# Pooled attention and MLP mixer on one core: column tiles for token tails, one more 7-product unit, more turns through HBM, K/V sums in two passes

## The chip, the core and the metric

The kernel runs on one core of a Trainium2 chip. TensorE (PE; its weight loads are PEld), VectorE (DVE), ScalarE (ACT), GpSimd (POOL) and SyncE (SP) each run their own instruction list in order and wait for each other through semaphores. The metric is the device time of one execution in microseconds (us).

## The reference

Eight batches; q, k, v of 8 heads, 576 rows, 64 columns. Attention against keys and values that are means over 8 rows, then a token mixer and a channel mixer:

```
k_p, v_p = mean over 8 rows of k, v                     # 72 rows each
attn = softmax(q @ k_p^T / sqrt(64)) @ v_p              # 576 x 64 per head
x = heads side by side                                  # 8 x 576 x 512
h = relu(x^T @ w_tok1) @ w_tok2                         # 576 -> 256 -> 576 over tokens
u = x + h^T
out = u + relu(u @ w_ch1) @ w_ch2                       # 512 -> 1536 -> 512
```

Inputs and output are float32; products run in bf16.

## The kernel before

The 576 tokens of a batch are split in 512 (4 chunks of 128) and a tail of 64. The channel mixer of the 512 runs in a *unit* per batch (units 0 to 7); the tails of all batches together make unit 8. A unit is a generator that yields every few matmuls; `PLANS[n]` lists, at each yield, which other steps are issued there: the attention and token mixer of the next batch, loads of later batches, sums. `HEAD` lists the steps before unit 0. The order of each engine's instructions is exactly this order of issue.

Names of the steps, for batch b:

- `lk lq lv` issue the loads from POOL's DMA queue. K and V of batches 1 to 3 come in one load as bf16. For batches from 4 on (`SUMMED = 4`), `+k` and `+v` (`add_rows`, L145) add further rows of a pooling group onto the first ones as the data land in float32: 4 passes of 2 rows each.
- `k0 k1 v0 v1` (DVE) and `K0 K1 V0 V1` (POOL) finish the pooled sums of half the heads, by `pool8` (L214 to L223: three additions) or for the summed batches one addition (L277). `kq0 kq1 vp0 vp1` do it on PE, as 8 matmuls with the identity that add up (L323).
- `kpT` transposes pooled K on PE and copies it out (L283, L285). `Q0 Q1` transpose q in 32 x 32 blocks on DVE (L345). `s0 s1 s2` are the scores (L357): four tiles of 32 rows of PE's array. `av0` to `av4` are attention times V (L391, L395, L396); `at0 at1` and `u0` to `u4` the token mixer (L453, L468, L470). `u4` does the tails of two batches at once: `w_tok2t` holds the tail's weights twice, padded with zeros, so that four matmuls of 128 x 128 weights fill two halves of one PSUM bank.
- u must then be turned for the channel mixer (`uT`). `t0` to `t3` (DVE evacuates) and `r0` to `r3` (ACT evacuates) do it by PE transposes, four per chunk (L480, L481). For batches from `BOUNCED = 6` on, `M0 M2` write u to HBM (L488), `M` reads it back in another order into the tile `v` (L494), both from SP, and `T0` to `T3` (L499) transpose blocks on DVE.

A unit's channel mixer has a first stage (`l1_tiles`, L561, relu on ACT L564) and a second. In units 0 and 1 the second stage is plain: 48 matmuls of 512 columns (L592). From `FAST = 2` on, the second stage is a Strassen-like form with 7 products of 12 matmuls of 256 columns (`unit_fast`, L777), which needs sums of blocks of w_ch2 (`W`, L664), sums of blocks of the relu output `GT` (`=`, `g_sums`, L614 and L625), and one DVE output per product (L799). In units 3 to 8 parts of the first stage are in such a form too (`first_fast`, L695), with sums of w_ch1 (`%`) and of uT (`^`, `token_sum`). All these sums run on DVE. `ps_one` has 4 PSUM banks, `ps_two` two pairs.

The head runs 26 matmuls on zeros (L862) ahead of batch 0's first transposes.

Of the kernel before, what the change touches and what calls it, by code (L numbers as in the profile page):

```python
# [14 lines left out]
SUMMED = 4  # L15
BOUNCED = 6
FAST = 2
# [11 lines left out]
PLANS = {  # L29
# [32 lines left out]
def kernel(  # L62
# [44 lines left out]
    w_tok2t = singles.tile([P, 2, 2, P], BF16)  # L107
# [29 lines left out]
    def pair_sums(b, key):  # L137
        return loaded[b, key].rearrange("j h i d -> j (h i d)").bitcast(FP32)[:, 0:H * 2 * D].rearrange(
            "j (h n) -> j h n", h=H)

    def add_rows(b, key):
        i = parts_of[b, key]
        parts_of[b, key] = i + 1
        src = (k if key == "k" else v)[b].rearrange("h (j i) d -> j h (i d)", i=POOL)
        nc.gpsimd.dma_start(out=pair_sums(b, key), in_=src[:, :, 2 * i * D:2 * (i + 1) * D],  # L145
                            accum_op=ALU.add if i else ALU.bypass)

    def load_kv(b, src, key):
        t = loaded[b, key] = raw.tile([SP, H, POOL, D], BF16, name=key + "r")
        if b >= SUMMED:  # L150
# [31 lines left out]
    def permute_tok2(m):  # L182
# [5 lines left out]
        for half in range(2):  # L188
            nc.gpsimd.tensor_copy(out=w_tok2t[:, :, half, half * BP:(half + 1) * BP], in_=w_tok2[:, :, 8 * BP:S])
# [48 lines left out]
    def batch_steps(b):  # L238
# [26 lines left out]
        def pool(eng, t, g):  # L265
            def go():
                hs = slice(g * HP, (g + 1) * HP)
                dst = st["kp"][:, g] if t == "k" else st["vp"][:, hs, 0:D]
                if b < SUMMED:
                    pool8(eng, loaded[b, t], hs, dst, t == "k")  # L270
                    return
                pair = pair_sums(b, t)[:, hs].rearrange("j l (i n) -> i j l n", i=2)
# [7 lines left out]
        def kpT():  # L280
# [4 lines left out]
            nc.vector.tensor_copy(out=st["kD"].rearrange("p g e j -> p (g e j)"), in_=ps.rearrange("p i j -> p (i j)"))  # L285
# [47 lines left out]
        def qT(hp):  # L333
            def go():
# [4 lines left out]
                nc.vector.tensor_copy(out=qT0[:, hp].rearrange("m l (r p) -> m r l p", p=BP), in_=ps)  # L339
# [118 lines left out]
        def u(c):  # L458
            def go():
                ps = ps_one.tile([P, 512], FP32, name="p1")  # L460
                if c < 4:
                    mms = [(w_tok2[:, m, c * P:(c + 1) * P], st["AT"][:, m, :]) for m in range(2)]
                    dst, x = late("u")[:, c, :], st["x"][:, c, :]
                else:
                    mms = [(w_tok2t[:, m, half, :], tails[b // 2, half][:, m, :]) for half in range(2) for m in range(2)]
                    dst, x = u_tails[:, b // 2, :], st["xt"]
                for i, (w, a) in enumerate(mms):
                    nc.tensor.matmul(out=ps, lhsT=w, rhs=a, start=(i == 0), stop=(i == len(mms) - 1))  # L468
# [54 lines left out]
        name = {"kpT": kpT}  # L523
# [11 lines left out]
        for hp in range(HP):  # L535
            name[f"kp{hp}"], name[f"kt{hp}"] = kp2(hp, False), kt2(hp, False)
            name[f"kP{hp}"], name[f"kT{hp}"] = kp2(hp, True), kt2(hp, True)
# [75 lines left out]
    def sub(out, a, b):  # L613
        nc.vector.tensor_tensor(out=out, in0=a, in1=b, op=ALU.subtract)  # L614

    def g_sums(s):
# [5 lines left out]
        if s[0] == "3":  # L622
            sub(S4[:, 2, f], GT[:, f, lo], GT[:, f, hi])
        elif s[0] == "1":
            nc.vector.tensor_tensor(out=S4[:, 0, f], in0=GT[:, f, hi], in1=GT[:, sec, hi], op=ALU.add)  # L625
        elif s[0] == "2":
            sub(S4[:, 1, f], S4[:, 0, f], GT[:, f, lo])
        else:
            sub(S4[:, 3, f], GT[:, sec, lo], S4[:, 1, f])
# [43 lines left out]
    def token_sum(n, u, i):  # L673
# [3 lines left out]
        sub(t[:, i], a, b)  # L677
# [92 lines left out]
    def unit_fast(n, u):  # L770
# [33 lines left out]
        def store_part(cols):  # L804
            def go(i):
                if i == 0:
                    return
                for half in range(2):
                    dst = out.rearrange("(c h) (p r) n -> h p c r n", h=2, r=BR)[half]
                    (nc.scalar if half else nc.sync).dma_start(out=dst[:, 2:4, 8, cols],  # L810
                                                               in_=ob[half * BP:(half + 1) * BP, :, cols])
            return go
# [23 lines left out]
        s2 = keep("s1")  # L836
        yield from product(x, lambda m: SG[:, 1, m], lambda m: TW[:, 1, m], False,
                           plus(s2, x, u1hi), last)
        if not last:
            w = bank()  # L840
            s4 = keep("s4")
            yield from product(w, lambda m: GT[:, NH + m, hi], lambda m: TW[:, 3, m], True, plus(s4, w, u2lo))
        yield from product(z, lambda m: SG[:, 3, m], lambda m: w_ch2[:, NH + m, hi], False, plus(oa[:, :, hi], z, s2))
        store(n, 0, oa)
        if last:
            yield from product(x, lambda m: SG[:, 2, m], lambda m: TW[:, 2, m], False,
                               plus(ob[:, :, hi], x, s5, store_part(hi)), True)
            yield from product(x, lambda m: GT[:, NH + m, hi], lambda m: TW[:, 3, m], False,
                               plus(ob[:, :, lo], x, u2lo, store_part(lo)), True)
# [118 lines left out]
```

## Time and profile before

| | |
|---|---|
| three runs | 270.61, 270.71, 271.94 us; median 270.71 |
| span of the profiled execution | 269.8 us (first to last instruction) |
| granted TensorE clock | 1.000 |
| PE, DVE, ACT, POOL busy | 259.5, 206.8, 122.7, 113.4 us |
| start of units 0 to 8 | 23.45, 58.85, 89.14, 119.1, 146.4, 175.3, 205.3, 226.9, 245.9 us |
| last matmul ends | 264.6 us |

The page gives no time of its own for the profiled execution beside its span; the median lies 0.9 us above the span. Busy time of PE includes the latency of a matmul, so the spacing of matmuls in the chain of waits is the better measure of their cost. Lines are numbered as in the kernel before.

### The profile page before, as it was taken

The page shows a single profiled execution, that of the slowest core. Times are in us where ns is not written, and L with a number is a line of the kernel's source. Part 1 is how long each engine was busy: PE and PEld are TensorE (multiplying, and loading weights), DVE is VectorE, ACT ScalarE, POOL GpSimd, SP SyncE. Part 2 cuts the span into 40 slices and gives each one's busy share as a digit, 9 for nine tenths or more (in the row PEclk, how much of TensorE's full clock was granted, in tenths as well). Part 3 has the DMA queues.
Part 4 walks back from the last instruction along what each step waited for, and adds up shares of the span by engine and source line. Part 5 has one row for each costly group of instructions (what it writes and reads, how often), then busy time and mean ns, then how long its engine had stood idle before and what let it go on. Part 6 is the DMA issues. An engine that isn't in the chain of part 4 may idle for free.

```text
span 269.8 us, 5432 instructions
## 1 busy us (share of the span) xinstructions
PE 259.5 (96%) x2173; PEld 171.7 (64%) x2200; DVE 206.8 (77%) x427; ACT 122.7 (45%) x207; POOL 113.4 (42%) x114
## 2 busy tenths in 40 slices
PE   8999999999999999999999999999999999999992
PEld 2776454545544645776587657864785688787781
DVE  4755573751798859996978798899799889997981
ACT  1375773047444353736563637264922632613600
POOL 5847749999995428636657242420000000000000
PEclk9999999999999999999999999999999999999999
DMA  7999999959969898998995997361506510404106
GB/s 184 190 194 205 204 212 204 180 126 190 153 132 140 154 159 118 146 169 168 155 141 83 156 213 87 39 164 40 119 0 147 149 18 21 137 2 116 41 2 157
DMA packets 42081, 35.17 MB, mean 130 GB/s; under 512 B 12040, under 2 KB 34408, under 8 KB 42056
## 3 DMA queue, kind: packets, MB, share of 16 engines
q0 software_dynamic: 30672, 22.11, 55.3%
q1 hardware_dynamic: 11056, 12.39, 17.2%
q10 hardware_dynamic: 328, 0.33, 0.5%
q8 instruction: 17, 0.28, 0.4%
q14 instruction: 8, 0.07, 0.1%
HBM read 36.90 MB, written 10.49 MB: 176 GB/s over the span
## 4 chain that ended last, share of the span: by engine, by line
PE 90%; DVE 5%; ACT 2%; issue 1%; DVEq 0%
PE p L777 24%; PE p L561 22%; PE p L695 9%; PE p L592 8%; PE p L453 6%; PE p L468 5%; PE p L357 4%; PE p L391 3%; PE p L862 3%; PE p L480 2%; PE p L323 1%; DVE area L614 1%; DVE u L470 1%; ACT ex L379 1%; ACT x L426 1%
## 5 line engine op out<-in xcount | busy, mean ns | idle before, releaser
L564 ACT ACTIVATE GT<-p 128x512 bf16<-128x512 f32 x76 | 44.5, 596 | 57.6 <-PE p L561 43.7
L561 PE MATMUL p<-uT,w_ch 128*128 128x512 bf16 x274 | 69.3, 380 | 0.9 <-issue 0.4
L561 PEld LDWEIGHTS <-w_ch 128*128 128x128 bf16 x304 | 32.4, 114 | 24.1 <-issue 1.7
L362 ACT ACTIVATE ex<-p 72x1024 bf16<-72x1024 f32 (+1 forms) x42 | 31.6, 804 | 27.5 <-PE p L357 27.3
L777 PEld LDWEIGHTS <-area 128*128 128x128 bf16 x336 | 31.9, 98 | 5.3 <-issue 1.3
L777 PE MATMUL p<-area,area 128*128 128x256 bf16 x252 | 30.8, 273 | 0.0
L145 POOL DMA_DIRECT2D kr<-in_k_dram x16 | 23.4, 1495 | 15.6 <-DMA kr<-in_k_dram 15.6
L145 POOL DMA_DIRECT2D vr<-in_v_dram x16 | 23.1, 1478 | 14.2 <-DMA vr<-in_v_dram 14.2
L470 DVE TENSOR_TENSOR u<-p,x 128x512 bf16<-128x512 f32 x32 | 21.1, 680 | 8.2 <-PE p L468 8.2
L777 PEld LDWEIGHTS <-GT 128*128 128x128 bf16 x252 | 24.2, 98 | 4.9 <-issue 0.6
L592 PE MATMUL p<-w_ch,GT 128*128 128x512 bf16 x92 | 23.6, 379 | 0.2
L777 PE MATMUL p<-w_ch,GT 128*128 128x256 bf16 x168 | 20.6, 273 | 0.1
L799 DVE TENSOR_TENSOR o<-p,s 128x512 f32<-128x512 f32 (+1 forms) x28 | 17.9, 662 | 3.2 <-PE p L777 3.1
L396 DVE TENSOR_TENSOR x<-p,den 128x512 bf16<-128x512 f32 x28 | 19.4, 691 | 1.0
L468 PE MATMUL p<-AT,w_tok 128*128 128x512 bf16 x62 | 17.3, 379 | 0.5 <-DVE u L470 0.5
L799 DVE TENSOR_TENSOR s<-p,u 128x512 f32<-128x512 f32 x24 | 16.2, 680 | 2.0 <-PE p L777 2.0
L395 DVE RECIPROCAL den<-p 128x8 f32<-128x8 f32 (+1 forms) x35 | 7.0, 201 | 11.3 <-PE p L391 10.9
L391 PEld LDWEIGHTS <-ex 72*128 72x128 bf16 x280 | 12.6, 98 | 3.9 <-DVE x L396 0.2
L592 PEld LDWEIGHTS <-GT 128*128 128x128 bf16 x96 | 8.8, 98 | 9.4 <-issue 0.4
L453 PE MATMUL p<-x,w_tok 128*128 128x512 bf16 x53 | 13.7, 379 | 0.2
L446 ACT ACTIVATE AT<-p 128x512 bf16<-128x512 f32 x14 | 8.4, 597 | 12.1 <-PE p L453 11.7
L391 PE MATMUL p<-vp,ex 72*128 72x65 bf16 x280 | 13.7, 194 | 0.0
(151 smaller groups left out, 448.8 us busy)
## 6 DMA issues: line engine op xcount, KB each, us to landing
out_dram<-o SPq DMA_DIRECT2D x34, 256.0 KB, 3.8
kr<-in_k_dram POOLq DMA_DIRECT2D x16, 288.0 KB, 7.4
vr<-in_v_dram POOLq DMA_DIRECT2D x16, 288.0 KB, 7.0
qb<-in_q_dram POOLq DMA_DIRECT2D x7, 576.0 KB, 10.1
kr<-in_k_dram POOLq DMA_DIRECT2D x3, 576.0 KB, 10.9
vr<-in_v_dram POOLq DMA_DIRECT2D x3, 576.0 KB, 12.4
w_ch<-in_moe_w_ch_dram POOLq DMA_DIRECT2D x6, 256.0 KB, 10.6
w_ch<-in_moe_w_ch_dram POOLq DMA_DIRECT2D x3, 512.0 KB, 13.1
```

Of the source, the lines that this page charges most:

```text
L145: nc.gpsimd.dma_start(out=pair_sums(b, key), in_=src[:, :, 2 * i * D:2 * (i + 1) * D], accum_op=ALU.add if i else ALU.bypass)
L362: nc.scalar.activation(out=exv[:, a, :, gs[0]:gs[-1] + 1, n0:n0 + n], func=AF.Exp, scale=scale, in_=pss[a][0:SP, :, 0:len(gs) * n].rearran ...
L391: nc.tensor.matmul(out=ps[:, h // 4, (h % 4) * (D + 1):(h % 4 + 1) * (D + 1)], lhsT=st["ex"][:, h * S + n0:h * S + n0 + P], rhs=st["vp"][: ...
L453: nc.tensor.matmul(out=ps, lhsT=w_tok1[:, c if c < 4 else 4 + par, m * P:(m + 1) * P], rhs=st["x"][:, c, :] if c < 4 else st["xt"], start= ...
L468: nc.tensor.matmul(out=ps, lhsT=w, rhs=a, start=(i == 0), stop=(i == len(mms) - 1))
L470: nc.vector.tensor_tensor(out=quads_of(dst, on), in0=plain_of(ps, on), in1=plain_of(x, on), op=ALU.add)
L561: nc.tensor.matmul(out=ps[m], lhsT=w_ch1[m // 4][:, kk, m % 4:512:4], rhs=moving(u)[kk], start=(kk == 0), stop=(kk == 3))
L564: nc.scalar.activation(out=GT[:, m, :], in_=ps[m], func=AF.Relu)
L592: nc.tensor.matmul(out=ps, lhsT=GT[:, m, c * P:(c + 1) * P], rhs=w_ch2[:, m, :], start=(m == 0), stop=(m == NM - 1))
L695: nc.tensor.matmul(out=ps[:, i], lhsT=w(i, k), rhs=mv(k), start=start and (i, k) == (0, 0), stop=stop and k == 1, skip_group_check=True)
L777: nc.tensor.matmul(out=ps[i] if split else ps[:, i], lhsT=a(m)[:, i * P:(i + 1) * P], rhs=w(m), start=start and m == 0 and (i == 0 or spli ...
L799: nc.vector.tensor_tensor(out=dst, in0=src, in1=other[:, i], op=ALU.add)
```

## The change

`BOUNCED` becomes 3 (batches 3, 4, 5 are turned through HBM too, in units 2, 3, 4), `FAST` becomes 1 (unit 1's second stage gets 7 products), and `ROWS` says that K and V of batches 4 to 7 are summed in 2 passes of 4 rows; one more addition then joins the halves. `PLANS` and `HEAD` are written anew, with batches named outright (`k1:2` is step k1 of batch 2); `#` is a GT sum on POOL instead of DVE, `~` a token sum on POOL, `kpA` is `kpT` with ACT evacuating, `p0` to `p3` are q transposes that ACT evacuates. K of batch 1 is pooled by `K0:1` (POOL, end of the head) and `k1:1` (DVE, unit 0), that of batches 2 and 3 by `k0 k1` (DVE, units 0 and 1). The head loads K and q in smaller alternating pieces from SP and has 13 matmuls on zeros. The second stage's products stand in a new order, and the last unit stores its results in smaller pieces.

```diff
-SUMMED = 4
-BOUNCED = 6
-FAST = 2
+ROWS = {4: 4, 5: 4, 6: 4, 7: 4}
+BOUNCED = 3
+FAST = 1
...
-HEAD = """z Z d2 Lc d5 d2 Lk8 d2 d2 d1 d2 d2 d1 d1 R0 c1 c0 I Lk1 Lq Lv0 Lv8 Lv1 kf0 Lf Lb La R1 d1 kf1 Bk1 H0 d1
-          d4 q1 kt0 kt1 q0 kp2 kp3 o0 e0 kt2 kt3 q2 q3 o1 e1 P0 vp0 o2 e2 a00 a01 a02 vp1 o3 e3 P1 y00 y01 y02 y03
-          y04 b10 X0 X1 a11 a12 A1 A0 y10 y11 y12 y13 y14 X2 X3 Bq1 Bv1 P2 H1 H2 Bk2 Ld G0"""
+HEAD = """Sk0 S80 z Sq0 Sk1 Sq1 N z0 R0 Z Lc d1 d1 d1 d1 d1 d1 d1 d1 d1 d1 d1 d1 d1 kf0 Lk1 c0 Lk8 Lv8 c1 Lv0 kf1
+          I kt0 p0 p1 e0 kt1 kp2 Lq La o1 Lv1 kP3 Lb Lf kt2 e1 Bk1 vp0 H0 o0 q2 Bq1 p3 kt3 a00 e2 e3 o2 a02 vp1 o3
+          a01 P1 b10 y00 X1 y01 y02 X0 a11 H1 y03 R1 y04 P0 y10 y11 X3 A1 a12 y12 A0 Bv1 y13 y14 X2 K0:1"""
...
+    1: {
+        3: "W00", 6: "W10", 7: "s1:2", 12: "lv:4 W02", 14: "lv:3 +k:4", 15: "W12 s2:2", 16: "W01", 18: "k0:3",
+        19: "k1:3 av1:2", 20: "av4:2", 21: "kpA:3", 22: "av3:2", 23: "lk:5 #3a",
+        24: "#3b r4:1 Q0:3 av0:2 #1a av2:2 =2a =1b", 26: "+v:4", 27: "Q1:3 W11 #2b", 28: "at1:2 at0:2 s0:3 =4b",
+        29: "u1:2", 30: "u3:2 W03", 32: "lq:5 s2:3", 33: "u0:2", 35: "r3:2 =4a s1:3", 37: "W13 u2:2", 39: "r1:2",
+        41: "r0:2 r2:2 V1:3 lq:4", 42: "V0:3",
+    },
...
+    3: {
+        0: "K1:5", 1: "~03", 4: "av0:4 av3:4", 7: "%31 ^13 K0:5", 8: "^23 ~33", 9: "lq:7 av4:4", 12: "at0:4",
+        13: "+v:6 =3a", 14: "at1:4", 15: "v1:5 kpA:5", 16: "u1:4 v0:5", 19: "u0:4 =3b =1a", 20: "s1:5 lk:6",
+        21: "u3:4 u2:4", 22: "#2a Q0:6 M0:4", 26: "=1b s0:5 =2b #4b", 28: "M2:4", 29: "Q1:6", 31: "#4a",
+        32: "M:4 av2:5", 33: "av0:5", 36: "T0:4", 37: "s2:5 T2:4", 38: "T3:4", 39: "T1:4 +k:6", 41: "lv:7 av4:5",
+        43: "av3:5",
+    },
...
-        nc.gpsimd.dma_start(out=pair_sums(b, key), in_=src[:, :, 2 * i * D:2 * (i + 1) * D],
+        nc.gpsimd.dma_start(out=pair_sums(b, key), in_=src[:, :, ROWS[b] * i * D:ROWS[b] * (i + 1) * D],
                             accum_op=ALU.add if i else ALU.bypass)
...
+                if ROWS[b] == 4:
+                    eng.tensor_tensor(out=rows[:, :, 0:2 * D], in0=rows[:, :, 0:2 * D], in1=rows[:, :, 2 * D:4 * D], op=ALU.add)
...
-                    mms = [(w_tok2t[:, m, half, :], tails[b // 2, half][:, m, :]) for half in range(2) for m in range(2)]
...
+                    for m in range(2):
+                        for half in range(2):
+                            nc.tensor.matmul(out=ps[rows2[half]], lhsT=w_tok2[:, m, 8 * BP:S],
+                                             rhs=tails[b // 2, half][:, m, :], start=(m == 0), stop=(m == 1),
+                                             tile_position=(0, half * BP))
...
-    def g_sums(s):
+    def g_sums(s, eng):
...
-    def token_sum(n, u, i):
+    def token_sum(n, u, i, eng):
...
-        yield from product(y, lambda m: GT[:, NH + m, lo], lambda m: w_ch2[:, NH + m, lo], True, plus(oa[:, :, lo], y, s1))
+        yield from product(y, lambda m: GT[:, NH + m, lo], lambda m: w_ch2[:, NH + m, lo], True,
+                           plus(oa[:, :, lo], y, s1, stored(0, oa, lo)))
+        s2 = keep("s1")
+        yield from product(x, lambda m: SG[:, 1, m], lambda m: TW[:, 1, m], False, plus(s2, x, u1hi), last)
         z = bank()
         s5 = keep("s5")
         yield from product(z, lambda m: SG[:, 0, m], lambda m: TW[:, 0, m], True, plus(s5, z, u2hi))
...
+        yield from product(x, lambda m: SG[:, 2, m], lambda m: TW[:, 2, m], False,
+                           plus(ob[:, :, hi], x, s5, stored(1, ob, hi)), last)
+        yield from product(z, lambda m: SG[:, 3, m], lambda m: w_ch2[:, NH + m, hi], False,
+                           plus(oa[:, :, hi], z, s2, stored(0, oa, hi)))
...
+        yield from product(x, lambda m: GT[:, NH + m, hi], lambda m: TW[:, 3, m], False,
+                           plus(ob[:, :, lo], x, u2lo, (lambda i: store_part(1, ob, lo, i)) if last else None), last)
```

More of the change, by code (lines that the diff above doesn't have):

```diff
@@ L187, in permute_tok2 @@
             return
-        for half in range(2):
-            nc.gpsimd.tensor_copy(out=w_tok2t[:, :, half, half * BP:(half + 1) * BP], in_=w_tok2[:, :, 8 * BP:S])
     def load_ch1(g):
@@ L802, in plus, with store_part @@
             return go
[L804 to L812, printed above, removed]
+        def store_part(g, o, cols, i):
+            for half in range(2):
+                dst = out.rearrange("(c h) (p r) n -> h p c r n", h=2, r=BR)[half]
+                (nc.scalar if half else nc.sync).dma_start(out=dst[:, 2 * g:2 * g + 2, 8, cols][:, i],
+                                                           in_=o[half * BP:(half + 1) * BP, i, cols])
         SG, TW = fast["S"], fast["T"]
@@ L835, in unit_fast @@
         yield from product(z, lambda m: SG[:, 0, m], lambda m: TW[:, 0, m], True, plus(s5, z, u2hi))
-        s2 = keep("s1")
-        yield from product(x, lambda m: SG[:, 1, m], lambda m: TW[:, 1, m], False,
-                           plus(s2, x, u1hi), last)
+        yield from product(x, lambda m: SG[:, 2, m], lambda m: TW[:, 2, m], False,
+                           plus(ob[:, :, hi], x, s5, stored(1, ob, hi)), last)
+        yield from product(z, lambda m: SG[:, 3, m], lambda m: w_ch2[:, NH + m, hi], False,
+                           plus(oa[:, :, hi], z, s2, stored(0, oa, hi)))
         if not last:
[L840 to L849, printed above, removed]
-        else:
-            def finish(i):
-                plus(ob[:, :, hi], x, s5)(i)
-                plus(ob[:, :, lo], x, s4)(i)
-            yield from product(x, lambda m: SG[:, 2, m], lambda m: TW[:, 2, m], False, finish)
+            store(n, 0, oa)
+        yield from product(x, lambda m: GT[:, NH + m, hi], lambda m: TW[:, 3, m], False,
+                           plus(ob[:, :, lo], x, u2lo, (lambda i: store_part(1, ob, lo, i)) if last else None), last)
+        if not last:
             store(n, 1, ob)
@@ L879, in head @@
             make_identity(nc, ident)
+        elif s[0] == "S":
+            a = int(s[2])
+            if s[1] == "q":
+                nc.sync.dma_start(out=qf[:, a:a + 1, :], in_=q_pairs(a, a + 1))
+            elif s[1] == "8":
+                kv(kf, k, 0, 0, HP, BP, SP, nc.scalar)
+            else:
+                kv(kf, k, 0, 2 * a, 2 * a + 2, 0, BP, nc.sync)
         elif s == "z":
             nc.vector.memset(warm, 0.0)
-            kv(kf, k, 0, 0, HP, 0, BP, nc.sync)
-            kv(kf, k, 0, 0, HP, BP, SP, nc.scalar)
-            for a in range(2):
-                nc.sync.dma_start(out=qf[:, a:a + 1, :], in_=q_pairs(a, a + 1))
+        elif s == "N":
             for key in "kqv":
                 load(key, 0)
+        elif s == "z0":
             nc.vector.memset(kpz, 0.0)
@@ L890, in head, with do @@
             nc.vector.memset(w_tok1[:, 4:6, :], 0.0)
-            nc.vector.memset(w_tok2t, 0.0)
         else:
             batches[0][1][s]()
+    def do(s):
+        if s[0] == "W":
+            weight_sum(int(s[1]), int(s[2]))
+        elif s[0] == "%":
+            in_weight_sum(int(s[1]), int(s[2]))
+        elif s[0] in "^~":
+            b = int(s[2])
+            token_sum(b, batches[b][2] if b < B else dict(uT=uT_tails), int(s[1]), nc.vector if s[0] == "^" else nc.gpsimd)
+        elif s[0] in "=#":
+            g_sums(s[1:], nc.vector if s[0] == "=" else nc.gpsimd)
+        elif ":" in s:
+            s, b = s.split(":")
+            if s[0] == "l":
+                load(s[1], int(b))
+            elif s[0] == "+":
+                add_rows(int(b), s[1])
+            else:
+                batches[int(b)][1][s]()
+        else:
+            head(s)
     def unit(n, at):
@@ L903, in unit @@
             for s in at.get(i, "").split():
[L904 to L930 removed]
+                do(s)
     with tc.manual_schedule(engines={PE, POOLE, DVE, ACT, SYNC}):
@@ L934 @@
         for s in HEAD.split():
-            head(s)
+            do(s)
         for n in range(B + 1):
```

91 lines of the change are left out of this document (43 added, 48 removed), and 50 rows, old and new, of the table PLANS.

## The prediction

> **What bounds the kernel now.** The page first: its busy shares and its chain of waits.
>
> ```profile
> PE 259.5 (96%) x2173; PEld 171.7 (64%) x2200; DVE 206.8 (77%) x427; ACT 122.7 (45%) x207; POOL 113.4 (42%) x114
> PE 90%; DVE 5%; ACT 2%; issue 1%; DVEq 0%
> ```
>
> TensorE (PE) carries 90% of the chain. VectorE (DVE) carries 5% and is the only other engine near its limit. Next the windows from unit to unit (columns: length, then busy time and count of PE, PEld, DVE, ACT, POOL; granted clock, DMA share, GB/s):
>
> ```profile
> 23.45:58.85 35.40, 34.79 (x253) 18.40 (x256) 20.79 (x39) 15.03 (x24) 27.44 (x25) 1.00 1.08 196
> 89.14:119.10 29.96, 29.25 (x253) 19.09 (x256) 25.77 (x51) 14.68 (x24) 17.21 (x15) 1.00 1.00 137
> 119.10:146.42 27.32, 27.17 (x255) 19.34 (x258) 21.52 (x44) 14.73 (x25) 16.28 (x17) 1.00 0.87 146
> 175.27:205.31 30.04, 29.93 (x273) 19.86 (x275) 28.01 (x57) 16.33 (x28) 1.60 (x2) 1.00 0.34 86
> ```
>
> PE is full in every unit at full clock. DVE reaches 28.0 of 30.0 us in unit 5 without stopping PE, so 93% of DVE is bearable. DMA is full up to unit 2. A busy PE counts latencies (380 ns for a 512-column matmul), so prices come from the chain in order of time, which shows spacings (start, length, what):
>
> ```profile
> 13.58 0.88 PE p L323 x8
> 57.54 0.45 PE p L480 x8
> 94.06 2.16 PE p L561 x10
> 100.41 1.27 DVE t L664
> 101.68 1.12 DVE area L614
> 217.43 9.17 PE p L777 x84
> ```
>
> 512 columns cost 216 ns, 256 columns 109, 128 columns 56. Counting the matmuls in both programs' instruction order at these prices (scores and AV by their own spacing, tail pairs as if free to overlap) gives 252.1 us before and 241.9 after. From the first matmul (1.2 us) to the last (264.6) are 263.4: 11.3 above the stream, 2.7 of them warm-ups at half pace, so only 8.6 us of PE time is waiting. The change takes 10.2 us of stream away, 2.8 of it warm-ups; what counts is how much comes back as new waits.
>
> **Part by part.** The sum starts from the profiled execution: span 269.8, to which 0.9 us is added so that it meets the median of 270.71.
>
> K of batch 1 off PE: 16 matmuls of 256 columns go, 16 x 109 = 1.74 us, in unit 0 where PE is full. In place come two DVE chains for halves of K (K1 and later ones) and one POOL chain (K0, at the head's end); the DVE chain is 1.21 + 0.69 + 0.42 = 2.32 us (L217, L218, L223 undisturbed). DVE takes five such K halves in units 0 and 1. By rows its load there is 30.5 + 24.9 against 43.4 before; PE's stream is 32.1 + 28.1. Covered, barely. The POOL chain (2.13 + 1.26 + 0.84 = 4.2 us) waits for K of batch 1 (landed at 20.9) and stands ahead of the loads of w_ch1's last third, w_ch2 and K of batch 2. The third landed at 32.5 to 34.8 with a 10 us queue before it, so an issue at 26 instead of 22 still finds that queue: nothing, or 2 us if it does not.
>
> Three more batches through HBM: 48 transposes go, 48 x 56 = 2.69 us. Their evacuations (5 on DVE at 0.42, 7 on ACT at 0.59) become 12 DVE block transposes at 0.67.
>
> 7-product stage in unit 1: 48 x 216 = 10.37 becomes 84 x 109 = 9.16: -1.21. DVE gets three more evacuations and the sums there.
>
> Column tiles for token tails: four times 4 matmuls of 512 columns (864 ns) become two pairs. No column tile is in this trace; the nearest row is the scores' row tiles, eight 512-column matmuls four at a time:
>
> ```profile
> 31.51 0.59 PE L561 MATMUL p<-uT,w_ch 128*128 128x512 bf16 x2
> 32.03 0.65 PE L357 MATMUL p<-qD,kD 32*72 32x512 bf16 x8
> 32.61 0.61 PE L468 MATMUL p<-AT,w_tok 128*128 128x512 bf16 x2
> ```
>
> From the second L561 matmul (31.72) to the first L357 one is 0.31 us where 0.216 is its own, and from there to L468 0.58 where two passes need 0.43: about 0.24 us to go in and out. So 0.43 + 0.24 = 0.67 per tail, -0.77 for four; bounds -1.73 (free switch) and +0.96 (no overlap). I take -0.77, the row of the same kind. The Trainium skill, TensorEngine Tiling (Array Packing), Key Properties, says that tiles work in parallel and that a change of tiling mode drains the array; by its first half alone the term would be -1.73, and the row agrees with the second half.
>
> New head: 13 warm-ups fewer. Before, the first real matmul came at 9.6, right after the 26th; all but the last q conversion (done at 8.6) had waited for them. Now PE could start near 7, but the first q transposes are evacuated by ACT, behind both conversions, so scores start near 9.5 instead of 11.5. Then w_ch1 gates unit 0 (landed 22.1 and 23.4; PE came at 23.45). Bounds -2.8 (all 13) and +1.0 (PE pauses and its clock falls); I take -1.0.
>
> Gains: 1.74 + 2.69 + 1.21 + 0.77 + 1.0 = 7.4 us.
>
> K/V sums in two passes: POOL issues 16 passes instead of 32 at 1.48 us each, 24 us back; one more add (DVE about 0.69, POOL 1.26) per half. Two landings of a 576 KB load (10.9 to 12.4) instead of four of 7.2: not later. POOL is off the chain: 0, bounds -1 and +1.
>
> Sums on POOL: 20 of 768 elements and 2 of 512 of the GT sums, 11 token sums. A POOL sum of 768 lies between L217 (1024 elements, 2.13) and L218 (512, 1.26): about 1.7 us where DVE takes 0.55. That is cheap on DVE's books, but look at both engines around 75 us:
>
> ```profile
> 33.86 1.21 DVE L217 TENSOR_TENSOR t<-vr 72x1024 f32<-72x1024 bf16 x1
> 74.04 2.14 POOL L217 TENSOR_TENSOR t<-vr 72x1024 f32<-72x1024 bf16 x1
> 75.14 1.46 DVE L614 TENSOR_TENSOR area<-w_ch 128x768 bf16<-128x768 bf16 x1
> 76.53 2.28 DVE L217 TENSOR_TENSOR t<-vr 72x1024 f32<-72x1024 bf16 x1
> ```
>
> While POOL adds, a DVE sum of two SBUF tiles takes about twice as long (1.46 for 0.55, 2.28 for 1.21); operations reading PSUM keep their time. The two rows at 100.41 and 101.68 are this too, on the chain. Now unit 3, the tightest. DVE by rows: 7 AV outputs 6.2, 4 u 2.7, 4 block transposes 2.7, 2 q transposes 1.5, V halves 2.2, sums 4.3, joins and relus 3.1, 7 product outputs 4.8, memsets 0.3: 27.8 us. In unit 4 of before the same sum gives 26.3 for 24.4 measured, so times 0.93: 25.9. Of this 6.5 is two-tile sums, with POOL adding 47% of the time: +3, so 28.9 against PE's 26.35. The other units come to 26.9 of 27.2 (2), 25.8 of 25.7 (4), 28 of 29.9 (5), 29.2 of 28.1 (1). In the units' last products DVE frees PE's PSUM banks, so an overhang stops PE. Bounds: 0 (absorbed over units) and +4; I take +1.3 in unit 3 and +0.5 in unit 1, half of each overhang. In unit 1 sums 3a, 3b, 1a and 2b also stand on POOL behind a load that waits for DVE's pooling of K 3, with 9.6 us of work for some 10 us of PE stream.
> The Trainium skill, GPSIMD Engine Reference, section 4.1, says elementwise work belongs on VectorE, GpSimd being about 2x slower with two inputs; here the ratio is 3. An estimate from that page would make a POOL sum 1.1 us and the 9.6 us 7.2, so unit 1 would cost nothing and the sum be -5.7.
>
> Bounce through HBM under load. Before, only batches 6 and 7 did it, in quiet DMA:
>
> ```profile
> out_dram<-o SPq DMA_DIRECT2D x4, 256.0 KB, 12.6
> mem<-u SPq DMA_DIRECT2D x4, 256.0 KB, 3.4
> v<-mem SPq DMA_DIRECT2D x8, 128.0 KB, 3.0
> ```
>
> (The first line is of 140 to 165 us, DMA crowded; all stores have a median of 3.8.) From the last u to turned tiles: 0.85 for u, 6.9 from the second write's issue (188.28) to the last landing (195.16), four block transposes 2.7: 10.4 us. PE's stream from the last u to the next unit's first matmul, which needs all of it, is 13.2, 11.4 and 14.6 us (batches 3, 4, 5; 17.5 and 18.1 for 6 and 7 before). Behind a block transpose that waits stand all of DVE's evacuations. On SP only output stores queue behind the reads; they have double buffers. I take +0.4, for batch 4; bounds 0 and +10.
>
> Costs: 1.3 + 0.5 + 0.4 = 2.2. Net -5.2: span 264.6, time 265.5.
>
> **Rivals.** Covers hold: no new wait, PE stays the only bound: -7.4, 263.3, and 260 if the head gives all and old waits shrink. For it: before, DVE ran at 93% with PE unharmed, and by rows its load in units 5 to 8 falls from 87.6 to 80.3 us.
>
> DVE becomes the bound: the doubling beside POOL stops PE by the full overhangs, 2.6 + 1.1 + 0.1, and by some 2 more in units 0 and 2, where the cover is 0.3 to 1: -7.4 + 3.8 + 2.0 + 0.4 = -1.2, 269.5. For it: at 99.7 to 107.3 of before, 7.6 us of DVE lie on the chain. Against: PE waited only 8.6 us in all. The Trainium skill, GPSIMD Engine Reference, section 1, says that GpSimd shares its SBUF interfaces with VectorE and contends with instructions of two SBUF inputs, which speaks for this rival; the rows at 75 us agree.
>
> Bounces late, and slower: units 2 to 4 load K, V and q of batches 5 to 7. The margins over the 10.4 us are 2.8, 1.0 and 4.2. One leg at 12.6 instead of 3.8 adds 8.8; at 6 us extra per batch the stalls are 3.2 + 5.0 + 1.8 = 10.0, and 265.5 - 0.4 + 10.0 = 275. It decides from about 4.4 us extra on, where 1.6 + 3.4 + 0.2 = 5.2 eats the net. Against: with only one or two K/V passes in flight (118 to 124 us) stores landed in 3.1 to 3.9.
>
> **Numbers.** Forecast 0.52 (262.5 to 268.5), covers hold 0.19, DVE bound 0.12, bounces late 0.17. Measurement tells 0.5%, 1.35 us, from no change. Faster: 0.52 + 0.19 and 0.02 of the DVE case, 0.73; within 0.5%: 0.07 of it; slower: 0.17 and 0.03, 0.20. Range 260 to 272.5: it leaves out most of the late-bounce case and little below.
>
> **What would show it.** Right: PE still about 90% of the chain; unit 0 starting near 22.5; no wait of DVE on v beyond 1 us; pairs of tail matmuls 0.67 us in all; DVE two-tile sums near 1 us beside POOL's. Wrong: block transposes that wait on v for several us, or a chain with DVE above 15%.

## The result, and the profile after

The changed kernel takes 297.05 us (median of 4, 296.29 to 298.05), the kernel before 270.66: 1.096 of its time, interval 1.092 to 1.099. The prediction was 265.5 us in 260.0 to 272.5. Ratios in this document use undisturbed runs alone, so they can differ from the ratio of the medians, which are of all runs; some runs of a1, a3, c1 and d2 were disturbed, the profiled one of a3 among them.

The page of the changed kernel: busy shares, the granted clock by fortieths of the span, and the chain of waits, which this time, followed back from the end, is lost after 14% of the span.

```profile
PE 259.4 (88%) x2133; PEld 172.9 (59%) x2159; DVE 224.3 (76%) x421; ACT 124.7 (42%) x212; POOL 130.2 (44%) x121
PEclk9779999999799999999995899958999999999999
PE 14%; DVE 0%; issue 0%
```

PE has the same busy time in a span that is 26 us longer, and the clock, full throughout before, falls in four places. The windows from unit to unit (length, then PE, PEld, DVE, ACT, POOL, clock, DMA share, GB/s; units 0, 1, 3, 4, 5):

```profile
26.61:61.14 34.53, 32.97 (x231) 15.88 (x235) 30.23 (x47) 14.08 (x25) 15.95 (x18) 1.00 1.03 184
61.14:94.79 33.65, 31.05 (x268) 19.51 (x271) 32.04 (x43) 19.52 (x32) 24.21 (x20) 0.95 0.98 157
...
123.97:162.49 38.52, 28.31 (x253) 19.58 (x255) 26.69 (x55) 12.61 (x21) 15.99 (x14) 0.89 0.73 149
162.49:199.49 37.00, 28.36 (x228) 18.45 (x228) 23.96 (x46) 13.80 (x23) 15.60 (x13) 0.87 0.52 106
199.49:231.28 31.79, 31.34 (x278) 20.64 (x280) 25.33 (x52) 15.94 (x27) 12.43 (x10) 0.96 0.25 67
```

Before, the same units took 35.24, 30.28, 27.30, 28.87 and 30.31 us. Units 3 and 4 lost 11.2 and 8.1, unit 1 3.4; the head lost 3.2 (unit 0 starts at 26.6, before at 23.45). The rest is within 1.5 us per unit and nearly cancels. The list of waits names what stands still in units 3 and 4 (waiter, what for, total us, times, longest):

```profile
PEld L808 <- issue: 24.8, 16, 10.2
DVE uT L530 <- DMA v<-mem: 20.9, 4, 10.4
PE p L808 <- DVE o L830: 18.7, 3, 10.1
```

DVE's block transposes (L530) wait 20.9 us for the reads of the turned sums. PE waits 18.7 for DVE evacuations (L830), which only queue behind those transposes. For batch 4, the timeline (start, us, engine, what, idle time before; SPq is SP's DMA queue):

```profile
145.21 2.69 SPq L525 DMA_DIRECT2D v<-mem  x4
...
146.01 1.40 POOL L169 DMA_DIRECT2D kr<-in_k_dram  x1
...
146.64 0.68 DVE L830 TENSOR_TENSOR s<-p,u 128x512 f32<-128x512 f32 x1
...
146.88 1.39 POOL L169 DMA_DIRECT2D vr<-in_v_dram  x1
...
157.75 0.71 DVE L530 STREAM_TRANSPOSE uT<-v 128x512 bf16<-128x512 bf16 x1 [10.43 <-DMA v<-mem]
158.38 0.65 DVE L830 TENSOR_TENSOR o<-p,s 128x512 f32<-128x512 f32 x1
```

POOL issues K 6's second pass and V 7's first in the middle of the four reads (K 6 is K of batch 6, a pass one of the two loads that sum it). The reads issued ahead of them landed after 2.5 and 3.2 us; the third, issued with V 7's pass, after 6.1, and the fourth at 157.62, 10.2 us after its issue. The passes themselves landed at 155.5 and 157.6. Batch 5 is the same with K 7's second pass (174.6) under its writes and V 7's (184.95) among its reads.

The stall has a second price. Windows of 2 us (same columns):

```profile
152.00:154.00 2.00, 0.00 (x0) 0.00 (x0) 0.00 (x0) 0.00 (x0) 0.00 (x0) 1.00 1.16 203
154.00:156.00 2.00, 0.00 (x0) 0.00 (x0) 0.00 (x0) 0.00 (x0) 0.00 (x0) 0.59 0.64 168
...
160.00:162.00 2.00, 2.00 (x17) 1.51 (x16) 1.94 (x5) 0.00 (x0) 1.02 (x1) 0.50 0.00 0
...
164.00:166.00 2.00, 2.00 (x16) 0.99 (x15) 0.27 (x2) 1.07 (x2) 1.99 (x3) 0.85 0.82 250
```

PE's last matmul ahead of the stall began at 148.8. By the shares of the windows the granted clock fell to 0.50 at 154.4 and rose at 164.6; PE was back at 159.1, so 5.5 us ran at half pace, some 2.7 us lost. Matmuls of 256 columns follow each other every 0.21 us there instead of 0.109. After batch 5's stall PE runs at half pace from 197 to 202; there the clock fell 3.3 us after PE had stopped, in batch 4's stall 5.4. The Trainium skill, TensorE: Matmul & The Clock Gate, Part 1 (What's actually happening), says that an idle window of about 3.4 us halves PE's clock and as long a busy one restores it; these rows agree in kind (3.3 and 5.4 us to fall, 5.2 and 5.5 to rise). In unit 1, below, the clock fell to 0.50 though PE's longest pause was 1.9 us.

In unit 1, DVE's and POOL's rows of the timeline:

```profile
67.98 0.69 DVE L240 TENSOR_TENSOR t<-t 72x512 f32<-72x512 f32 x1
...
68.70 5.52 DVE L243 TENSOR_TENSOR kp<-t 72x256 bf16<-72x256 f32 x1
...
69.10 3.25 POOL L645 TENSOR_TENSOR area<-GT 128x768 bf16<-128x768 bf16 x2
...
72.31 1.62 POOL L656 TENSOR_TENSOR area<-GT 128x768 bf16<-128x768 bf16 x1
```

The last addition of pooling K 3 takes 0.42 us undisturbed. Here POOL started three additions back to back 0.4 us later, and DVE ended 0.3 us after the third: held, not slowed to half. The plan makes the two meet: ahead of POOL's three additions stands a load that waits for DVE's first addition of this half of K 3. PE waited 1.9 us for DVE's sum and ran at 0.50 from 76 to 79.

The head, PE by time:

```profile
1.19 4.44 PE L887 MATMUL p<-area 128*128 128x512 bf16 x13 [1.19 <-DVE area L914]
7.47 0.29 PE L338 MATMUL p<-ident,area 72*128 72x72 bf16 x4 [1.83 <-POOL ident masks.py:199]
...
10.60 0.67 PE L318 MATMUL p<-kr,ident 72*72 72x128 bf16 x8 [1.22 <-DMA kr<-in_k_dram]
```

PE stops for POOL's identity and again for K, and the clock is 0.50 from about 11 to 18 us.

The first tail, by time (start, us; the four column-tile matmuls are the middle row):

```profile
60.01 0.65 PE L384 MATMUL p<-qD,kD 32*72 32x512 bf16 x8
60.58 0.62 PE L497 MATMUL p<-AT,w_tok 128*64 128x512 bf16 x4
61.14 0.84 PE L592 MATMUL p<-uT,w_ch 128*128 128x512 bf16 x2
```

From the first tail matmul to the next product are 0.555 us in all four tails, and some 0.09 more lie ahead of them: 0.65.

### The profile page after: what moved, and what is told of

It is laid out like the page before. It is cut to its first block, busy times and chain, and to the rows that moved or that the text cites. A ratio compares the mean times of both kernels' runs of the same rounds, so it can differ in the third digit from the quotient of the medians.

```text
span 295.5 us, 5417 instructions
## 1 busy us (share of the span) xinstructions
PE 259.4 (88%) x2133; PEld 172.9 (59%) x2159; DVE 224.3 (76%) x421; ACT 124.7 (42%) x212; POOL 130.2 (44%) x121
## 5 line engine op out<-in xcount | busy, mean ns | idle before, releaser
L592 PEld LDWEIGHTS <-w_ch 128*128 128x128 bf16 x304 | 32.3, 115 | 26.2 <-issue 4.9
L808 PEld LDWEIGHTS <-GT 128*128 128x128 bf16 x288 | 28.6, 103 | 28.7 <-issue 22.6
L808 PEld LDWEIGHTS <-area 128*128 128x128 bf16 x384 | 36.4, 98 | 8.6 <-issue 2.3
L808 PE MATMUL p<-area,area 128*128 128x256 bf16 x288 | 35.3, 273 | 0.6 <-DVE area L645 0.6
L808 PE MATMUL p<-area,GT 128*128 128x256 bf16 x96 | 14.6, 307 | 18.7 <-DVE o L830 18.7
L530 DVE STREAM_TRANSPOSE uT<-v 128x512 bf16<-128x512 bf16 x20 | 13.1, 688 | 20.9 <-DMA v<-mem 20.9
L645 POOL TENSOR_TENSOR area<-GT,area 128x768 bf16<-128x768 bf16 x8 | 13.3, 1681 | 27.0 <-DVE area L645 27.0
L808 PE MATMUL p<-w_ch,GT 128*128 128x256 bf16 x192 | 25.0, 281 | 0.0
L830 DVE TENSOR_TENSOR o<-p,s 128x512 f32<-128x512 f32 (+1 forms) x25 | 16.2, 652 | 3.1 <-PE p L808 2.7
L645 POOL TENSOR_TENSOR area<-area,GT 128x768 bf16<-128x768 bf16 x4 | 6.8, 1700 | 23.6 <-DVE area L656 13.4
L645 POOL TENSOR_TENSOR t<-uT 128x512 bf16<-128x512 bf16 x5 | 5.7, 1152 | 25.8 <-DVE uT L530 14.4
L645 POOL TENSOR_TENSOR area<-GT 128x768 bf16<-128x768 bf16 (+1 forms) x8 | 12.1, 1522 | 10.3 <-DVE GT L738 6.5
L830 DVE TENSOR_TENSOR s<-p,u 128x512 f32<-128x512 f32 x21 | 14.4, 684 | 1.7 <-PE p L808 1.6
## 6 DMA issues: line engine op xcount, KB each, us to landing
kr<-in_k_dram POOLq DMA_DIRECT2D x11, 576.0 KB, 10.6
vr<-in_v_dram POOLq DMA_DIRECT2D x11, 576.0 KB, 10.7
```

The source lines that it names most:

```text
L530: nc.vector.transpose(out=late("uT")[:, :, c * P:(c + 1) * P].rearrange("f (k e) (a t) -> f a k e t", e=2, a=4), in_=st["v"][:, 4 * c:4 * ...
L592: nc.tensor.matmul(out=ps[m], lhsT=w_ch1[m // 4][:, kk, m % 4:512:4], rhs=moving(u)[kk], start=(kk == 0), stop=(kk == 3))
L645: eng.tensor_tensor(out=out, in0=a, in1=b, op=ALU.subtract)
L808: nc.tensor.matmul(out=ps[i] if split else ps[:, i], lhsT=a(m)[:, i * P:(i + 1) * P], rhs=w(m), start=start and m == 0 and (i == 0 or spli ...
L830: nc.vector.tensor_tensor(out=dst, in0=src, in1=other[:, i], op=ALU.add)
```

## The experiments

**First: undo one thing each.** Four kernels made from the changed one. (Edits are shortened; `...` stands for steps that stay.) a1 turns batches 3 to 5 on PE again:

```
-BOUNCED = 3
+BOUNCED = 6
-  25: "... M0:3 u4:3", 26: "%11 M2:3 ...", 30: "#3a M:3", 36: "T0:3", 38: "T1:3 T3:3 T2:3"
+  25: "... u4:3", 26: "%11 ...", 30: "#3a", 36: "r0:3", 38: "r1:3 r3:3 r2:3"     # 4 and 5 alike
```

> The changed kernel with one part undone: batches 3 to 5 are turned by TensorE transposes again (in the same steps of the plan), only 6 and 7 through HBM. Theory 'late bounces' (the two PE waits of 10.2 and 8.5 us at 148.8 and 188.3 us are DVE's block transposes standing behind reads of the turned sums that the DMA queues deliver late): units 3 and 4 go from 38.5 and 37.0 us to 28 to 30 each, of which 1.8 us is the transposes coming back; the other units stay within 1 us; 297 becomes 278 to 281 us. Rival 'DVE is held by POOL' (units 3 and 4 are long because sums on POOL stop DVE): units 3 and 4 stay above 34 us, the total above 288.

Measured: 277.86 us (273.8 to 280.1), ratio 1.013 (1.006 to 1.019). Units 3 and 4 take 27.6 and 28.3 us. Late bounces it is; POOL's sums are all still there.

a2 keeps the bounces and takes passes away:

```
-  39: "T1:4 +k:6", 41: "lv:7 av4:5"        # unit 3
+  39: "T1:4", 41: "av4:5"
-  11: "at1:5 ~24" ... 20: "+k:7" ... 28: "+v:7"   # unit 4
+  11: "at1:5 ~24 lv:7"
```

> The changed kernel with all three bounces kept, but without what runs on the DMA engines beside those of batches 4 and 5: the second accumulating passes of K of batches 6 and 7 and of V of batch 7 are left out (those sums lack half their rows), and the first pass of V of batch 7 is issued in unit 4's step 11. Theory 'collision' (the turn is late because its small packets share the DMA engines with an accumulating pass): DVE's waits on v fall from 21 us to below 4, units 3 and 4 come to 28 to 30 us each, the total to 278 to 281. Rival 'the turn is too long for its place' (issue, write, read and four block transposes do not fit between the last u and the next unit, whatever else is on the queues): the waits stay at 7 to 10 us each and the total above 290.

Measured: 279.94 us, 1.031 (1.027 to 1.034). The waits fell from 20.9 us to this, a little over what was expected:

```profile
DVE uT L530 <- DMA v<-mem: 5.6, 3, 3.3
```

Unit 4 took 26.7 us, less than with PE's transposes. Unit 3 took 31.0 us and kept a wait of 3.3: batch 4's write still meets V 6's second and K 6's first pass (7.1 us to land instead of 2.2). So in unit 4 the turn fits its place when no pass is there.

a3 moves all of POOL's sums to DVE (each `#` to `=`, each `~` to `^`):

> The changed kernel with all 22 GT sums and 11 token sums that POOL makes moved to DVE, in the same steps. Theory 'POOL holds DVE for its whole addition' (a DVE sum of two SBUF tiles of 0.42 us took 5.52 beside three POOL additions): the time that DVE loses beside POOL falls from 15.4 us to about 6, what is left being POOL's K pooling; unit 1 goes from 33.65 to 31 to 32 us. DVE gets some 33 sums of 0.5 us more and loses as much waiting. The bounces still set units 3 and 4, so the total is 293 to 297 us. Rival, the prediction's 'twice as long beside POOL' (POOL really takes work off DVE): DVE's load grows by some 16 us less 5, unit 1 stays or grows, total 298 to 303.

Measured: 311.09 us, 1.137 (1.131 to 1.142): slower than the changed kernel by 4% (1.137 against 1.096), outside both expectations. Units 2, 3 and 4 of it:

```profile
98.53:143.94 45.41, 31.19 (x249) 19.22 (x248) 27.73 (x50) 13.05 (x21) 13.36 (x12) 0.82 0.86 158
143.94:183.63 39.69, 28.91 (x256) 19.79 (x254) 26.87 (x56) 12.60 (x21) 10.57 (x10) 0.89 0.56 120
183.63:211.64 28.01, 27.33 (x231) 17.79 (x228) 24.87 (x52) 13.91 (x23) 0.00 (x0) 0.97 0.29 77
```

POOL, with no sums to make, came to its passes earlier. V 6's second and K 6's first (123.7, 124.5 us) now met batch 3's reads, which did no harm in the changed kernel and now landed after 7 to 14 us: PE waited 12.4 us in unit 2 and 10.7 in unit 3. In unit 4 no pass was left and batch 5's reads took 2.5 to 3.3. The stall follows the passes. It also means that the plan's steps do not say when a load starts; POOL's own work does. In this plan the sums were the pacing.

a4 makes the 13 warm-ups 26 again (`d1` to `d2`, 13 times):

> The changed kernel with 26 warm-up matmuls again instead of 13, everything else of its new head kept. Theory 'the clock falls in the pause' (PE stops for 2 us before the identity is ready, and again for ACT and DMA; the granted clock is 0.83 over the first 20 us and the first plain product runs at half pace): the gap is filled, the clock of the first 20 us is above 0.9, unit 0 starts at 23.5 to 24.5 instead of 26.6 us, total 294 to 295. Rival 'the new order of the head is late by itself' (ACT conversions and POOL's identity and K pooling set the start, the clock does not matter): unit 0 starts at 26 to 28 us, total 296.5 to 298.5.

Measured: 294.99 us, 1.085 (1.080 to 1.090), 2.06 less. PE by time:

```profile
1.20 8.06 PE L887 MATMUL p<-area 128*128 128x512 bf16 x26 [1.20 <-DVE area L914]
9.09 0.30 PE L338 MATMUL p<-ident,area 72*128 72x72 bf16 x4
```

No stop ahead of the identity, clock 1.00 over the first 20 us, unit 0 at 24.0 us. The clock theory holds. But the clock does not fall in every execution: in a1's profiled run, also with 13 warm-ups, it was 1.00 all through the head, and unit 0 started at 23.3 us.

**Second: unit 1.** The base b0 is a1 and a4 together.

> The changed kernel with two parts undone at once: batches 3 to 5 turned by TensorE, and 26 warm-up matmuls. It is the base of the next three. From the first run's units (34.9, 33.6, 30.0, 27.6, 28.3, 30.5, 40.0 for two, 23.8 us, sum 248.6) and the head of the fourth (24.0): span 272.7, time 273 to 275.5, with less spread than the 273.8 to 280.1 of the first run if the head is what spreads there. If the two effects do not add (the long head of the first run was not the clock), it stays near 277 to 278.

Measured: 275.66 us (275.3 to 276.7), 1.014 (1.009 to 1.020). The time is near the expected range and the spread is gone. That the two parts add is not shown: by the ratios the base is level with a1 (1.014 and 1.013), and in a1's profiled run the head had lost nothing.

b1 takes K of batch 1 back to PE:

```
-HEAD: "... X2 K0:1"      0: "u0:0 A2:0 A3:0", 3: "k1:1"
+HEAD: "... X2"           0: "u0:0 A2:0 kq0:1 A3:0 kq1:1"
```

> The base, with K of batch 1 summed by TensorE again (16 matmuls of 256 columns in unit 0, no sum of it on POOL or DVE). Theory 'PE carries it' (the prediction's): unit 0 grows by the 1.74 us of its matmuls, the total by 1.2 to 1.8. Theory 'DVE pays': unit 0 has 30 us of DVE work in 35, and a DVE K sum held by POOL (2.8 us for 0.42) is what PE waits for in it, so unit 0 grows by less than 0.7 or becomes shorter, total within 0.7 us of the base.

Measured: 276.73 us, 1.017 (1.011 to 1.024): 1.07 slower, between the two expectations; the intervals overlap. In the profiled runs unit 0 grew by 0.4 us only (36.3 against 35.9), as 'DVE pays' has it. With K off PE, PE waits 2.3 us in it, 1.4 for u, which stands behind a held DVE sum, and 0.9 for w_ch; with K on PE it waits 1.3, for u. The held sum belongs to K 2, so it stayed.

b2 moves unit 1's four POOL sums to DVE (`#3a #3b #1a #2b` to `=`).

> The base, with the four sums that POOL makes in unit 1 (3a, 3b, 1a, 2b) moved to DVE, nothing else. Unit 1 is 33.6 us where before had 30.3. Theory 'POOL holds DVE': the last step of DVE's pooling of K 3 takes 0.42 us instead of 5.5, PE's wait of 1.95 us for it goes, its clock stays at 1.00 behind it, and unit 1 comes to 31 to 32.3 us although DVE has four sums (2.2 us) more; total 1.3 to 2.5 less than the base. Rival 'DVE is simply full in unit 1' (32.0 of 33.6 us busy): the four sums come on top, unit 1 is 33.5 to 35.5 us.

Measured: 277.00 us, 1.019 (1.012 to 1.025). Unit 1: 34.3 us, as in the base. The K sum is free of the hold, as expected, but V 3's pooling on POOL moved up in POOL's queue and held other DVE sums: 6.1 us of unit 1 instead of 9.6. The time is the rival's; whether its reason holds, a full DVE, is asked again in c4.

b3 makes unit 1 plain again (`FAST = 2`, unit 1's eight sums left out of its plan).

> The base, with unit 1 by plain products again (48 of 512 columns in place of 84 of 256, and none of unit 1's eight sums), the rest as it is. Theory 'the 7-product stage costs unit 1 more on DVE and POOL than it saves on PE': unit 1 comes to 30.3 to 31.3 us, the total 2.3 to 3.3 below the base. Rival 'the new order of loads and poolings is what makes unit 1 long': unit 1 grows by the 1.2 us of PE stream to 34 to 35.

Measured: 271.75 us, 1.000 (0.998 to 1.003). Unit 1: 30.0 us. With this all that the change lost is undone; 3.9 us of it is the 7-product stage with its sums. Nothing is gained either, though K of batch 1 off PE and the column tiles are still in.

c4 takes b2 and gives DVE V 3's pooling too (`V1:3 V0:3` to `v1:3 v0:3`):

> The base (TensorE turns batches 3 to 5, 26 warm-ups) with unit 1's four POOL sums and both halves of V 3's pooling on DVE, so that POOL adds next to nothing beside unit 1's products. Undisturbed, DVE's work of unit 1 is then 22.5 + 4 x 0.55 + 2 x 2.32 = 29.3 us. Theory 'unit 1 is long because POOL holds DVE' (9.6 us of 32.1 in the base, 6.1 of 30.6 with only the sums moved): the held time in unit 1 falls below 1.5 us, and although DVE does 6.8 us more, unit 1 comes to 31.5 to 33 us. Theory 'DVE has too much to do in unit 1, held or not': unit 1 stays at 33.5 us or more, total 276 to 279.

Measured: 274.91 us, 1.013 (1.009 to 1.017). Unit 1 in the base, and here:

```profile
59.68:93.97 34.29, 31.01 (x269) 19.33 (x272) 32.07 (x44) 19.52 (x32) 24.24 (x20) 0.95 0.98 155
59.16:89.46 30.30, 28.98 (x269) 18.55 (x272) 27.32 (x49) 19.41 (x32) 13.85 (x14) 1.00 1.14 175
```

DVE is busy 4.8 us less although it does more, and the unit is 4.0 us shorter, more than expected; 2.0 us are still held. But V 3 comes late and PE waits 1.7 us for it in unit 2. Units 1 and 2 together: 64.3 in the base, 62.2 here, 60.0 with a plain unit 1. By these profiles the hold is about half of what unit 1 lost. The times do not show it: c4's runs lie between 273.7 and 276.2 us, the profiled one is the fastest of the four, and the ratio is the base's (1.013 and 1.014). The rest contains V 3's lateness and what is still held; DVE's work as such was not separated from them.

**Third: keep the bounces and move the passes.** c1 has a plain unit 1, 26 warm-ups, all bounces, and its passes elsewhere:

```
 unit 2: 25: "lv:6" -> 33: "+v:5 lv:6"
 unit 3: 20: "lk:6" -> 0: ; 13: "+v:6" -> 7: ; 39: "+k:6" -> unit 4, 8: "~04 +k:6 lk:7"; 41: "lv:7" -> unit 4, 39:
 unit 4: 20: "+k:7" -> 39: "~05 +k:7 lv:7"; 28: "+v:7" -> unit 5, 3: "+v:7 K1:7"; K 6, K 7, V 7 summed later
```

> The changed kernel with all three bounces, 26 warm-ups and a plain unit 1, and with the passes moved out of the bounces: V 6's first pass behind unit 2's last POOL sum, K 6's first pass and V 6's second into the first third of unit 3, K 6's second and K 7's first into the start of unit 4 (behind a token sum that needs the turned tiles, so they cannot start sooner), K 7's second and V 7's first behind the last turn of unit 4, V 7's second into unit 5; batch 7's scores and AV follow later. Everything is computed. Theory 'collision': no wait on v beyond 2 us, units 3 and 4 27 to 28 and 26.5 to 27.5 us (without late passes unit 4 came to 26.7 where TensorE's transposes make it 28.3), total 268 to 270.5, faster than the base with a plain unit 1 (271.75). Rival 'every place in units 2 to 5 is somebody's bounce' (the moved passes and q of batches 6 and 7 meet other reads or make scores late): one or more waits of 3 us or more, total 272 to 280.

Measured: 292.06 us, 1.074 (1.070 to 1.078). Every read of batches 3, 4 and 5 landed in 2.5 to 3.6 us, so collision holds for the reads. On v DVE waited 3.4 us in all, 2.6 of it in unit 3, where a write of batch 4 took 5.7 us beside V 6's second pass and q of batch 7; unit 3 took 29.5 us, unit 4 32.2. K 6's second pass landed 13.1 us after its issue and K 7's at 190.5, and PE waited for pooled K: twice 2 us in unit 4, 8.3 us at one place in unit 5, which took 43.7. The total lies beyond both expectations, and the rival had half of the mechanism: no read was hit, but there was no room left for the loads.

c3 is c1 with `u0:1` ahead of `k0:2` in unit 0; `k0:2` also moves from step 31 to 33, behind two loads.

> The run before it in this call, with one more edit in unit 0: u 0 of batch 1 ahead of DVE's pooling of the last half of K 2, which a POOL addition holds (2.8 us for 0.42) and for which TensorE waits 1.5 us at 52 us. If that wait is the hold's, it goes: 0.8 to 1.5 us less than the run before it. If the pooling then makes the transposes of K 2 late instead: within 0.5 us of it.

Measured: 291.71 us, 1.075 (1.072 to 1.079), no change; PE's transposes of K 2 wait 1.6 us for its last sum instead.

c2 is the kernel before with the column tiles alone (L497's four matmuls in place of L468's):

> The kernel before with one part of the change alone: the four token tails as pairs of column tiles (the second copies of the weights are still made, but not used). The prediction counted 0.67 us per tail instead of 0.864, the changed kernel's trace shows 0.645: 4 x 0.22 = 0.88 us less, ratio 0.9968. If entering and leaving the tiles cost nothing: 1.73 less, 0.9936. If the two tiles did not overlap: 0.9 more, 1.0035.

Measured: 271.49 us, 0.9995 (0.997 to 1.002). The time cannot tell 0.88 us from nothing; the trace shows 0.65 to 0.72 us per tail instead of 0.864.

**Fourth: one bounce at a time, on b3.** d1 turns batch 3 through HBM and issues V 6's first pass behind unit 2's last POOL sum; d2 differs in one place:

```
 d1:  25: "=2a =1b s2:4 M0:3 u4:3",               33: "+v:5 lv:6 =4a s0:4"
 d2:  25: "=2a lv:6 +v:5 =1b s2:4 M0:3 u4:3",     33: "=4a s0:4"
```

> The base with a plain unit 1 (TensorE turns batches 4 and 5, 26 warm-ups; it took 271.75 us), with batch 3 turned through HBM and V 6's first pass issued behind unit 2's last POOL sum, so that no pass starts between the write of batch 3's sums and the end of their reads. Theory 'collision, and a clean bounce pays': reads of 2.5 to 3.5 us, unit 2 at 28.3 us as with the moved passes (30.0 with TensorE's transposes), the other units as in the base: 269.5 to 270.5. Rival 'the bounce only moves the time' (DVE's block transposes or the later pass lengthen unit 3): 271.3 or more.

> The run before it in this call with one thing changed: V 6's first pass and V 5's second stand ahead of unit 2's POOL sum 3a instead of behind sum 4b. The same instructions, every sum complete. Theory 'collision': the reads of batch 3's turned sums land 7 to 14 us after their issue instead of 3, DVE waits for v, units 2 and 3 together grow by 3 to 9 us. Rival 'the turn's length in the changed kernel comes from something other than the passes' place': within 1 us of the run before it.

Measured: d1 269.68 us, 0.995 (0.993 to 0.997); d2 278.65 us, 1.025 (1.020 to 1.031). POOL's issue of the two passes and DVE's first block transpose of each, d1 first:

```profile
112.25 2.26 POOL L169 DMA_DIRECT2D vr<-in_v_dram  x2
...
114.76 0.69 DVE L530 STREAM_TRANSPOSE uT<-v 128x512 bf16<-128x512 bf16 x1
```

```profile
104.57 2.29 POOL L169 DMA_DIRECT2D vr<-in_v_dram  x2
...
121.92 0.71 DVE L530 STREAM_TRANSPOSE uT<-v 128x512 bf16<-128x512 bf16 x1 [5.16 <-DMA v<-mem]
```

And the DMA view of 103 to 123 us (KB each, median us to landing), d1 first:

```profile
v<-mem SPq DMA_DIRECT2D x4, 128.0 KB, 3.3
```

```profile
v<-mem SPq DMA_DIRECT2D x4, 128.0 KB, 11.9
```

With the same instructions, the place of two passes makes the reads 3.6 times as long and unit 2 37.9 us instead of 28.3 in the profiled runs; the ratios differ by 3%. Units 2 and 3 together grew by 10.4 us there, more than expected. For the last part of d2's reads a third load, q of batch 6, was in flight too (issued at 113.3). The move has one more effect: POOL's sum behind the two issues starts later and holds a DVE sum for 3.6 us (at 105.3), for which PE stands 2.0 us and runs 3.4 us at half pace. PE still reaches its stall at 118.8, and the reads land at 121.7, so it is they that set the unit's end. And a bounce that is left alone pays: unit 2 is 1.7 us shorter than with PE's transposes, and d1 beats the kernel before by 0.5%.

d3 turns batch 5 too, with K 7's second pass behind unit 4's last sum (`20: "+k:7"` to `28: "+k:7 +v:7"`):

> The first run of this call with batch 5 turned through HBM too; K 7's second pass is issued with V 7's behind unit 4's last POOL sum, and token sum 3 of batch 5 goes ahead of K 7's pooling on POOL. Theory 'a clean bounce pays': reads of 2.5 to 4 us, unit 4 at 26.5 to 27.2 us instead of 28.3, unit 5 within 0.5 us: 268 to 269.3. Rival 'K 7 becomes late' (as with the moved passes, where K summed late cost units 4 and 5 some 17 us): TensorE waits for kp in unit 5, total 271 to 276.

Measured: 269.80 us, 0.9955 (0.994 to 0.997): no gain over d1, and above the range expected. Unit 4 is 26.2 us, 2.1 less, as the theory has it; K 7 is not late. In the profiled run unit 6 gives 1.7 of it back: DVE waits 2.1 us for the reads of batch 7's sums, which were issued 4.0 us after that batch's second write instead of 2.2. Why that write landed late was not tried.

## Why the prediction was wrong, step by step

One path through the runs, part by part: 271.75 (b3), 3.9 for unit 1's products (b0), 19.3 for the bounces (a4), 2.1 for the warm-ups: 297.05. Such a path adds up by itself; another order can share the time out differently.

**Bounce through HBM, +0.4: the step that failed.** With the transposes that it saves, the turn was to gain 2.3 us; it cost 19.3, far beyond the bound of +10 too. Its rival, bounces late and slower, names the mechanism, the margins and the queue behind the block transposes rightly, and had 0.17. What decided against it was the sentence that stores landed in 3.1 to 3.9 us with one or two passes in flight. That row is of stores, at one place; reads beside two passes took up to 10.2 us here, 11.9 (median) in d2. The row of 12.6 us, taken as the far bound, was nearer. The rival's own size (10.0) was short too: stalls of 10.2 and 8.5, and twice about 2.7 at half clock. Batch 3, with a margin of 2.8, was not hurt: its reads took 6.3 to 6.8 us.

The step also did not ask when POOL would come to each pass. K 6's second pass stands at step 39, behind the bounce's block transposes, but it was issued at 146.0, between the reads, as soon as POOL's last sum was done. a3 and d2 show that this decides. Whether shorter passes, of 2 rows as before, would have hit the reads as hard was not tried.

**48 transposes, -2.69:** right where nothing collides: -1.7 for batch 3 (unit 2), -2.1 for batch 5 (unit 4), more than the 0.9 each of the transposes themselves; with them goes PE's wait for their evacuation by ACT, 1.1 us in unit 4.

**7 products in unit 1, -1.21 and +0.5:** measured +3.9. What failed here is "about twice as long" beside POOL. It came from a DVE sum that took 1.46 us at 75.14 beside a POOL addition from 74.04 to 76.18; that it ended 0.4 us after POOL did, most of its undisturbed 0.55, was not seen. A sum is held until POOL's addition ends, and three additions without a gap held one for 5.1 us. The base lost 9.6 us so in this unit; for unit 3 I had counted 3. The Trainium skill, Trainium Architecture — The Big Picture, What this means for kernel authors, calls the port pair of VectorE and GpSimd an exclusive lock and no split of bandwidth; the rows agree, and it would have priced this better than the section that I cited. How much of the 3.9 is the hold stays open: with most of it gone (c4), the profiled units 1 and 2 are still 2.1 us longer than with plain products, and the time of all runs is the base's.

**New head, -1.0:** wrong in sign. The bad bound named the mechanism ("PE pauses and its clock falls") and priced it at +1.0; the 13 warm-ups alone were worth 2.1 here, though the clock does not fall in every execution (a1). With 26 warm-ups unit 0 starts at 23.4 to 25.2 us over the runs, so the new order gains nothing either.

**Column tiles, -0.77:** right: 0.65 per tail against 0.67. **K of batch 1, -1.74:** not shown; 1.07 by the medians with overlapping intervals, 0.4 in unit 0. "Covered, barely" did not hold: 1.4 us of new wait for u stand behind a held DVE sum, 0.9 for w_ch. These two terms promised 2.5 us, and b3, which keeps both, is level with the kernel before. **Two passes, 0:** their landing time was right (median 10.6 us); what a pass of 10 us does to others in flight was not asked.

**DVE's overhang in unit 3, +1.3:** not settled. With the bounces undone unit 3 took 27.6 us, before 27.3, but there DVE has no block transposes to do (2.7 us). With clean reads in unit 3 (c3) PE waited 0.5 us in it for a DVE sum and 0.8 behind block transposes that waited on v; but there POOL adds less than in the changed kernel (11.6 us against 16.0).

The signs named in advance worked: "block transposes that wait on v for several us" is the list of waits above.

## What to carry to other kernels

A step that leaves an engine through DMA and comes back is as short as the traffic beside it: find out what else is in flight between its write and its last read, by when the issuing engine will really reach each transfer and not by its place in a plan, and make a large transfer wait for something that ends after the round trip. Taking work off a busy engine can also take away the thing that kept a queue from running ahead. Price a stall of PE of some us with the half pace that follows it.

## What the runs showed of the hardware that was not expected

- Reads of 128 KB from HBM on SP's queue: 3.3 us alone, 11.9 beside two loads of 576 KB from POOL's queue, and for the last part a third (medians, d1 and d2, the same kernel but for the order). Writes of 256 KB: 2.2 alone, 7.1 beside two.
- A DVE addition of two SBUF tiles that has begun waits until POOL's addition ends, and through three that follow each other without a gap: 5.52 us for 0.42. Where 0.1 us lies between POOL's additions, it got through behind the first (2.79 us for 0.42 at 51.6, beside one of 2.13).
- The granted clock is 1.00 or 0.50; windows between them hold a change. It fell 3.3 and 5.4 us after PE had stopped and rose 5.2 and 5.5 us after it was back; in unit 1 a stretch of 4 us in which PE was busy for half was enough.
